# Pooled attention and a gated convolution on one core: the division cut in two, the scale moved into the keys, and a new order for every engine

## The chip, the core and the metric

The kernel runs on one core of a Trainium2 chip. Its engines are TensorE (PE, with its weight loads shown as PEld), VectorE (DVE), ScalarE (ACT), GpSimd (POOL) and SyncE (SP), each with its own program that it works off in order; semaphores join them, and DMA queues are fed from POOL, SP and ACT. The metric is device time in microseconds, the median of several runs. Matmul results land in PSUM, which this kernel uses as eight banks of 128 x 512 fp32.

## What is computed

Eight batches, each with eight heads of 576 rows of 64. Keys and values are averaged over groups of eight rows (72 are left), each query row is scored against the 72 pooled keys of its head, and the softmax of the scores weights the pooled values. The heads side by side are a 576 x 512 activation per batch, which goes through a gated network:

```python
k_p = k.reshape(B, H, Sp, 8, D).mean(axis=3); v_p = v.reshape(B, H, Sp, 8, D).mean(axis=3)
scores = scale * np.matmul(q, k_p.transpose(0, 1, 3, 2))          # scale = 1 / sqrt(64)
attn = np.exp(scores - np.max(scores, axis=-1, keepdims=True))
attn = attn / (np.sum(attn, axis=-1, keepdims=True) + 1e-09)
x = heads_side_by_side(np.matmul(attn, v_p))                      # (8, 576, 512)
h = np.maximum(x @ w_in, 0.0)                                      # (8, 576, 1024)
conv_out = sum(conv_w[k] * shifted(h, k - 1) for k in range(3))    # along the 576 rows
out = (h * sigmoid(conv_out)) @ w_out                              # (8, 576, 512)
```

Inputs and output are fp32 in memory; the kernel computes in bf16 with fp32 sums.

## The kernel before

Batches go in four groups of two (g = 0 to 3). A batch has 576 rows, nine chunks of 64, so a group is cut into nine tiles of 128 query rows (group 0, whose batches are kept apart at the seam, into ten). In the text below b is a batch, t a tile, fb one of eight blocks of 128 of the 1024 hidden columns, f4 a half of these.

*Loads.* POOL issues one casting DMA after another (q in `load_q`, L272; v L305 and L308; keys of a whole group L279; w_in L315, w_out L323). The first batch's keys and part of its queries come raw through SP (L287) and are cast by DVE and ACT (L294). Buffers are few (one for keys, four for q, three for v), so an issue waits until the buffer's former content has been read, and the rest of POOL's queue waits behind it.

*Preparation.* For batches 0 and 1, PE pools the keys with a matrix `pm` of ones (L406, L416). For the others DVE adds the eight rows (`pool_pair`, L439) and PE turns the sums with `pick`, a rearranged identity (L445), or with `ident` itself in the last group (L468). ACT or DVE copies the result out of PSUM into `kT`. PE turns the queries (L516, L520) and ACT or DVE copies them into `qT` (L534); the last group's are turned by DMA. DVE pools the values (L486, L490) into `vm`, beside which a column of eights gives the row sums.

*Attention of one tile.* `att_scores` on PE (L582 in 64 x 64 pieces, L595 in 128 x 128), the row maxima on DVE (`att_max`, L608), the shift by the maximum (`att_shift`, on PE L628 in group 0, on DVE L620 in the others), the exponential on ACT (`att_exp`, L646) with the factor 1/64 as its scale, a turn on PE with a copy (L657, L671) or by DMA (L666), the product with the values on PE (`att_values`, L682). Its result fills two PSUM banks: eight heads of 64 columns and a sum each. `att_divide` on DVE then takes the reciprocals of the eight sums (L695) and multiplies (L697), which frees the two banks. A turn on PE and a copy (L714, L722), or a DMA, puts the tile into `xT`.

*The network of one batch.* PE makes a block of 128 hidden columns (`ffn_in`, L727, eight matmuls of 288 columns into two banks), ACT takes the relu of half of it (L736). The convolution runs along the rows in one of two ways: on PE (`ffn_conv`, L889, pieces of 64 x 64 with diagonal matrices) followed by a tanh on ACT (L914); or, for the pairs (b, f4) in `TAPS`, as three taps: ACT the middle one (L862), DVE the two outer ones (L864), ACT the tanh (L869). With tanh for the sigmoid, DVE adds one and multiplies by `hT`: `ffn_gate` (L925, L927) and `ffn_times` (L935) on the first way, both in `ffn_tap_gate` (L875, L876) on the second. PE multiplies with w_out (`ffn_out`, L943, eight matmuls of 512 columns a tile), ACT or DVE copies (L954), SP or ACT stores (L966).

*What sets the order.* Nothing is ordered by the code's loops. They call `add(...)`, which makes a list of some 900 steps, each with the engines that may do it. Three tables then fix everything: `ORDER` is the sequence of the steps (a step's number doubled, plus one where its second engine does it, so that a copy may be ACT's or DVE's; -1 is a fill, a matmul on a zeroed tile whose result nobody reads, L399), `FORMS` tells whether scores and turns are cut into small pieces, and `PLACES` which buffer or PSUM bank a step gets. `tg`, the accumulator of the taps, has three buffers, `e` six, `x` four.

```python
for n in self.ORDER:
    o = spares.pop(0) if n < 0 else self.ops[n // 2]
    o.engine = list(o.engines)[0 if n < 0 else n % 2]
```

## Time and profile before

| | us |
|---|---|
| median of 3 runs | 217.13 (217.02 to 217.79) |
| span of the profiled execution | 216.5 |
| its time outside the span | not given; the runs' median is 0.63 above the span |
| PE busy (matmuls) | 201.9 |
| DVE busy | 193.2 |
| ACT busy | 162.7 |
| POOL busy | 41.5 |

Durations below are from that one profiled execution; busy time is the union over an engine's instructions. A matmul that waits in PE's queue counts as busy, so 93% of PE is not PE at its peak. Lines of groups read: line, engine, operation, tiles, shapes, count, then busy us, mean ns of one, then idle time of the engine just before them and what ended most of it. In lists of instructions by time the first two numbers are the start and the length in us, and the bracket holds the idle time before and what ended it. In the chain of waits the numbers are start and length.

### The profile page before, as it was taken

To read this page: it belongs to the slowest core of one execution; us is meant where nothing else is said; L and a number is where in the kernel's file an instruction comes from. 1 tells how busy PE (TensorE), PEld (TensorE's weight loads), DVE (VectorE), ACT (ScalarE), POOL (GpSimd) and SP (SyncE) were. 2 spreads that over 40 slices of the span, in tenths; PEclk is the share of its full clock that TensorE was granted. 3 is DMA by queue.
4 is the path that set the end of the run, shared out by engine and by line. 5 is a ranking of instruction groups with operands and counts; after the bars stand their busy time and mean duration, and the time that the engine had idled before them with its cause. 6 is when DMAs were issued, how large, how long until landed. Compare 5 with 4: busy or idle time off the path is not lost.

```text
span 216.5 us, 6617 instructions
## 1 busy us (share of the span) xinstructions
PE 201.9 (93%) x2753; PEld 137.0 (63%) x2753; DVE 193.2 (89%) x334; ACT 162.7 (75%) x278; POOL 41.5 (19%) x78
## 2 busy tenths in 40 slices
PE   7599999969999999999999899989999999999992
PEld 3557778855788776766776675665656666654451
DVE  7598989999999999999999799999899999998621
ACT  2548885896998887787497594878979999997420
POOL 8644330050052101000000030002201210370000
PEclk9799999999999999999999999999999999999999
DMA  6999999999999999969687634576347745602685
GB/s 210 227 207 209 206 207 208 210 205 206 207 205 206 154 153 179 158 164 165 131 111 100 136 74 89 58 156 148 78 104 153 158 100 123 145 0 51 169 242 171
DMA packets 48833, 33.46 MB, mean 155 GB/s; under 512 B 28300, under 2 KB 43812, under 8 KB 48804
## 3 DMA queue, kind: packets, MB, share of 16 engines
q0 software_dynamic: 15216, 15.40, 43.5%
q1 hardware_dynamic: 32512, 16.13, 36.6%
q10 hardware_dynamic: 1076, 1.52, 2.5%
q8 instruction: 21, 0.34, 0.7%
q14 instruction: 8, 0.07, 0.1%
HBM read 32.52 MB, written 9.44 MB: 194 GB/s over the span
## 4 chain that ended last, share of the span: by engine, by line
PE 45%; DVE 34%; issue 6%; ACT 6%; DMA 5%; SPq 2%; DVEq 0%
PE psum L943 20%; PE psum L727 16%; DVE negm L608 7%; DVE x L697 6%; DVE sd L620 4%; DVE gT L935 4%; DMA hT<-in_k_dram 3%; DVE v L486 3%; DVE gT L927 3%; PE psum L889 2%; DMA out_dram<-osb 2%; DVE r L695 2%; PE psum L682 2%; ACT e L646 2%; DVE gT L925 1%
## 5 line engine op out<-in xcount | busy, mean ns | idle before, releaser
L727 PE MATMUL psum<-xT,w_in_sb 128*128 128x288 bf16 x512 | 74.1, 286 | 2.2 <-DMA xT<-x 1.1
L943 PE MATMUL psum<-w_out_sb,gT 128*128 128x512 bf16 (+1 forms) x296 | 69.5, 374 | 0.7 <-DVE gT L935 0.6
L727 PEld LDWEIGHTS <-w_in_sb 128*128 128x128 bf16 x512 | 47.9, 98 | 19.1 <-issue 2.0
L736 ACT ACTIVATE hT<-psum 128x576 bf16<-128x576 f32 x64 | 40.3, 650 | 14.0 <-PE psum L727 13.4
L943 PEld LDWEIGHTS <-gT 128*128 128x128 bf16 x296 | 27.3, 98 | 26.5 <-issue 0.9
L864 DVE SCALAR_TENSOR_TENSOR tg<-hT,convw,tg 128x576 f32<-128x576 bf16 x48 | 37.6, 815 | 0.5
L608 DVE TENSOR_REDUCE negm<-psum 128x8 f32<-128x576 f32 (+2 forms) x37 | 27.5, 752 | 2.3 <-PE psum L582 1.6
L697 DVE TENSOR_TENSOR x<-psum,r 128x512 bf16<-128x512 f32 (+1 forms) x37 | 25.6, 691 | 1.4
L811 POOL COPY hT<-hT 128x126 bf16<-128x126 bf16 x16 | 7.5, 467 | 97.6 <-ACT hT L736 80.1
L620 DVE TENSOR_TENSOR sd<-psum,negm 128x576 f32<-128x576 f32 x27 | 20.2, 753 | 0.5
L682 PE MATMUL psum<-vm,eT 128*128 128x130 bf16 (+5 forms) x240 | 18.9, 222 | 1.1 <-DVE x L697 0.7
L646 ACT ACTIVATE e<-sd 128x576 bf16<-128x576 f32 x27 | 18.2, 685 | 1.3 <-DVE sd L620 1.1
L954 ACT COPY osb<-psum 128x512 f32<-128x512 f32 x27 | 15.7, 585 | 4.4 <-PE psum L943 4.2
L889 PE MATMUL psum<-hT,dw 64*64 64x288 bf16 (+2 forms) x608 | 18.7, 261 | 0.1
L682 PEld LDWEIGHTS <-eT 128*128 128x128 bf16 (+1 forms) x240 | 15.3, 100 | 5.4 <-DMA eT<-e 1.2
L862 ACT ACTIVATE tg<-hT,convw 128x576 f32<-128x576 bf16 x24 | 18.1, 772 | 0.1
L889 PEld LDWEIGHTS <-dw 64*64 64x64 bf16 x608 | 14.8, 107 | 4.6 <-issue 3.7
L869 ACT ACTIVATE gT<-tg 128x576 bf16<-128x576 f32 x24 | 16.3, 683 | 0.7 <-DVE tg L864 0.5
L914 ACT ACTIVATE gT<-psum 128x576 bf16<-128x576 f32 x20 | 12.9, 651 | 3.9 <-PE psum L889 2.7
L914 ACT ACTIVATE tg<-psum 128x576 bf16<-128x576 f32 x20 | 13.0, 652 | 2.6 <-PE psum L889 1.4
L935 DVE TENSOR_TENSOR gT<-gT,hT 128x2304 bf16<-128x2304 bf16 x10 | 13.5, 1352 | 0.1
L486 DVE TENSOR_TENSOR v<-v 128x1280 bf16<-128x1280 bf16 (+2 forms) x24 | 13.0, 540 | 0.2
(84 smaller groups left out, 234.2 us busy)
## 6 DMA issues: line engine op xcount, KB each, us to landing
out_dram<-osb SPq DMA_DIRECT2D x54, 128.0 KB, 2.4
v<-in_v_dram POOLq DMA_DIRECT2D x8, 512.0 KB, 13.1
qp<-in_q_dram POOLq DMA_DIRECT2D x7, 576.0 KB, 14.4
kk<-in_k_dram POOLq DMA_DIRECT2D x3, 1152.0 KB, 14.6
out_dram<-qp ACTq DMA_DIRECT2D x10, 128.0 KB, 2.7
hT<-in_k_dram SPq DMA_DIRECT2D x2, 576.0 KB, 5.0
w_in_sb<-in_moe_w_in_dram POOLq DMA_DIRECT2D x2, 512.0 KB, 14.2
w_out_sb<-in_moe_w_out_dram POOLq DMA_DIRECT2D x1, 1024.0 KB, 24.7
```

What stands on the lines that cost most here:

```text
L608: nc.vector.tensor_reduce(out=a["m"][0:rows], in_=a["s"][0:rows, :, 0:2 * KW].rearrange("p a (h s) -> p a h s", s=Sp), axis=AX.X, op=OP.ma ...
L620: nc.vector.tensor_tensor(out=a["d"][0:rows], in0=a["s"][0:rows, :, 0:2 * KW].rearrange("p a (h s) -> p a h s", s=Sp), in1=a["m"][0:rows]. ...
L646: nc.scalar.activation(out=dst, in_=src, func=ACT.Exp, scale=1.0 / (POOL * 8.0),)
L682: nc.tensor.matmul(out=a["o"][lo:hi, h // 4, (h % 4) * (D + 1):(h % 4 + x1 - x0) * (D + 1)], lhsT=a["eT"][:, j, lo:hi], rhs=buf("vm", b)[: ...
L697: nc.vector.tensor_tensor(out=a["x"][0:rows].rearrange("p (a h d) -> p a h d", a=2, d=D), in0=ov[:, :, :, 0:D], in1=r[0:rows].unsqueeze(3) ...
L727: nc.tensor.matmul(out=banks(ps)[:, j, 0:SC], lhsT=w_in_block(dc, fb), rhs=buf("xT", g)[:, dc, i * S + j * SC:i * S + (j + 1) * SC], start ...
L736: nc.scalar.activation(out=h_of(b)[:, fb].rearrange("p (a s) -> p a s", a=2), in_=banks(ps)[:, :, 0:SC], func=ACT.Relu, scale=0.5,)
L864: nc.vector.scalar_tensor_tensor(out=acc, in0=h, scalar=w, in1=acc, op0=OP.mult, op1=OP.add)
L889: nc.tensor.matmul(out=banks(pss[r ^ c])[c * D:(c + 1) * D, j, lo:hi], lhsT=dw[r * D:(r + 1) * D, tap * n_fb + fb, :], rhs=hT[r * D:(r + 1 ...
L914: nc.scalar.activation(out=t.rearrange("p (a s) -> p a s", a=2), in_=banks(ps)[:, :, 0:SC], func=ACT.Tanh, scale=0.5,)
L935: nc.vector.tensor_tensor(out=gate, in0=gate, in1=h_of(b)[:, four], op=OP.mult)
L943: nc.tensor.matmul(out=bank(ps)[0:rows, columns], lhsT=buf("gT", g)[:, fb, t * P:t * P + rows], rhs=w_out_sb[:, fb, columns], start=(fb == 0),
```

## The change

- `att_divide` becomes two steps. `att_invert` takes the reciprocals on DVE; the multiply is a step of its own, which DVE does as before or ACT does as eight activations of 64 columns, one a head, each with its reciprocal as scale. `ORDER` gives four of the 37 multiplies to ACT.
- `ffn_tap_gate` keeps only the addition of one; the product becomes a step of its own (`ffn_times`).
- The factor 1/64 leaves the exponential. The pooling matrix is filled with it in place of 1.0, and a scaled identity `ident_k` (one more small DVE instruction) is what `pick` is made of and what the last group's keys are turned with.
- `ORDER`, `FORMS` and `PLACES` are new throughout. There are 40 fills for 17, 21 of them ahead of PE's first real matmul (14 before). Of the first batches' turns and scores, other ones are cut small: 252 small query turns for 216, 336 small score pieces for 320. DVE copies two of the large `qT` blocks (five before), ACT eight (five).
- A variant of the exponential, eight activations with the maximum as bias, is added but used nowhere (`EIGHT` is empty).

```diff
@@ class Graph
+    EIGHT = ()
     ORDER = (
-        0, 10, 12, 24, 16, -1, 4, 44, -1, 28, 8, -1, 36, -1, 14, -1, -1, 32, -1, -1,
...
+        0, 10, 24, 16, 4, 44, 28, 8, 36, 12, 14, 32, 46, 3, -1, -1, -1, -1, -1, 48,
...
@@ constants
+    KSCALE = 1.0 / (POOL * 8.0)
+    ident_k = const.tile([P, P], BF16, name="ident_k")
@@ clear_pool_matrix
-        nc.vector.memset(pm[0:TB, :, 0:Sp], 1.0)
+        nc.vector.memset(pm[0:TB, :, 0:Sp], KSCALE)
@@ build_pick
+        nc.vector.tensor_scalar(out=ident_k, in0=ident, scalar1=KSCALE, scalar2=None, op0=OP.mult)
...
-                    in_=ident.rearrange("p (s a hh f e) -> p s a hh f e", s=2, a=2, hh=2, f=2)[:, :, :, hh, f],
+                    in_=ident_k.rearrange("p (s a hh f e) -> p s a hh f e", s=2, a=2, hh=2, f=2)[:, :, :, hh, f],
@@ turn_keys
-                    rhs=ident[:, i * D:(i + 1) * D],
+                    rhs=ident_k[:, i * D:(i + 1) * D],
@@ att_exp
             func=ACT.Exp,
-            scale=1.0 / (POOL * 8.0),
@@ division
+    def att_invert(g, t):
+        nc.vector.reciprocal(out=buf("r", g, t)[0:rows_of(g, t)], in_=att_heads(g, t)[:, :, :, D])
+
+    def att_divide(g, t, engine):
...
+        if engine == "ACT":
+            for n in range(H):
+                nc.scalar.activation(
+                    out=a["x"][0:rows, n * D:(n + 1) * D],
+                    in_=ov[:, n // 4, n % 4, 0:D],
+                    func=ACT.Identity,
+                    scale=r[0:rows, n // 4, n % 4:n % 4 + 1],
+                )
+            return
@@ ffn_tap_gate
         nc.vector.tensor_scalar(out=gate, in0=gate, scalar1=1.0, scalar2=None, op0=OP.add)
-        nc.vector.tensor_tensor(out=gate, in0=gate, in1=h_of(b)[:, four], op=OP.mult)
@@ add_att
-        o = add(dve(0.2, 0.69), key, lambda: att_divide(g, t), after=[o], uses=[x, rr, big])
+        o = add({"DVE": 0.115}, key, lambda: att_invert(g, t), after=[o], uses=[rr, big])
+        o = add({"DVE": 0.61, "ACT": 0.82}, key, None, after=[o], uses=[x, rr, big])
+        o.emit = lambda o=o: att_divide(g, t, o.engine)
@@ add_ffn
-            gated = add(dve(0.78, 1.39), w, lambda f4=f4: ffn_tap_gate(b, f4), after=tanh, uses=[htok[b], gtok[g]])
+            o = add(dve(0.78), w, lambda f4=f4: ffn_tap_gate(b, f4), after=tanh, uses=[gtok[g]])
+            gated = add(dve(1.39), w, lambda f4=f4: ffn_times(b, f4), after=[o], uses=[htok[b], gtok[g]])
```

The lines of the changed kernel are shifted, by 10 to 34; the reciprocal is L716 there, the multiply L731 on DVE and L724 on ACT, the pooling steps L450 and L497, the relu L770. Three places of the order:

DVE in group 1, before: after the first pooling step of the next group's keys (L439 `kk`), two divisions, each reciprocal (into `r`) ahead of its multiply (into `x`), then the maximum of another tile (`negm`) and its shift (`sd`).

```order
L439 TENSOR_TENSOR kk_76<-kk_76 128x9x256
L695 RECIPROCAL r_111<-psum 128x8
L697 TENSOR_TENSOR x_108<-psum,r_111 128x512
L695 RECIPROCAL r_109<-psum 128x8
L697 TENSOR_TENSOR x_105<-psum,r_109 128x512
L608 TENSOR_REDUCE negm_95<-psum 128x8
L620 TENSOR_TENSOR sd_127<-psum,negm_95 128x576
```

The same place now:

```order
L450 TENSOR_TENSOR kk_77<-kk_77 128x9x256
L716 RECIPROCAL r_110<-psum 128x8
L716 RECIPROCAL r_111<-psum 128x8
L731 TENSOR_TENSOR x_106<-psum,r_110 128x512
L692 COPY eT_103<-psum 128x640
...
L619 TENSOR_REDUCE negm_96<-psum 128x8
L631 TENSOR_TENSOR sd_128<-psum,negm_96 128x576
```

The two reciprocals stand ahead of the first multiply, and the second multiply (of `r_111`) is no longer on DVE. It is on ACT, while batch 1's relus (into `hT`) and the last tanh results of batch 0 (into `gT`, `tg`) run; before, ACT had at that place

```order
L914 ACTIVATE tg_118<-psum 128x576
L914 ACTIVATE gT_119<-psum 128x576
L722 COPY xT_113<-psum 128x4x128
L736 ACTIVATE hT_115<-psum 128x576
L671 COPY eT_104<-psum 128x640
```

and now

```order
L946 ACTIVATE gT_120<-psum 128x576
L946 ACTIVATE tg_119<-psum 128x576
L770 ACTIVATE hT_116<-psum 128x576
L756 COPY xT_114<-psum 128x4x128
L724 ACTIVATE x_108<-psum,r_111 128x64 x8
L770 ACTIVATE hT_116<-psum 128x576
L668 ACTIVATE e_99<-sd_127 128x576
```

The eight activations of one division stand between two relus, whose PSUM banks PE waits for.

POOL's queue at the start, before: keys and q of batch 1, four clears of the ends of `hT`, w_in's first half, q of batch 2, w_in's second half, v of batch 1.

```order
L272 DMA qp_72<-in_q_dram 128x4x320
L305 DMA v_85<-in_v_dram 128x4x512
...
L272 DMA kk_76<-in_k_dram 128x4x576
L272 DMA qp_73<-in_q_dram 128x4x576
L806 MEMSET hT_114 128x8
...
L315 DMA w_in_sb_66<-in_moe_w_in_dram 128x4x512
L272 DMA qp_74<-in_q_dram 128x4x576
L315 DMA w_in_sb_67<-in_moe_w_in_dram 128x4x512
```

Now:

```order
L282 DMA qp_74<-in_q_dram 128x4x320
L315 DMA v_87<-in_v_dram 128x4x512
...
L282 DMA kk_77<-in_k_dram 128x4x576
L282 DMA qp_74<-in_q_dram 128x4x576
L282 DMA qp_73<-in_q_dram 128x4x576
L325 DMA w_in_sb_67<-in_moe_w_in_dram 128x4x512
L325 DMA w_in_sb_68<-in_moe_w_in_dram 128x4x512
```

The clears have gone far back, q of batch 2 stands ahead of both halves of w_in, and q of batch 1 goes into the buffer that q of batch 0 has (`qp_74`; two buffers before), so its issue, with all behind it, waits until PE has turned batch 0's queries.

More of the change, by code (lines that the diff above doesn't have):

```diff
@@ L1113, in add_pair @@
             t = token("ps", n=2)
-            o = add({"PE": 0.26}, key, lambda b=b, t=t: turn_keys(b, t), after=[prev, c0], uses=[t, kk[g]], mode=HALF, count=36)
+            o = add({"PE": 0.26}, key, lambda b=b, t=t: turn_keys(b, t), after=[prev, picked], uses=[t, kk[g]], mode=HALF, count=36)
             c = add(either(0.76, 0.71), key, None, after=[o], uses=[t, ktok[b]])
@@ L1209, in add_att @@
         o = add(dve(0.75), key, lambda: att_max(g, t), after=[o], uses=[ng, s])
-        if shift_by_dve(g, t):
+        if by_head(g, t):
+            o = add({"ACT": 0.9}, key, lambda: att_exp(g, t), after=[o], uses=[e, s, ng, lim])
+        elif shift_by_dve(g, t):
             sd = token("sd", g, t)
@@ L1340, in add_out @@
             key += nudge("ot", 9 * g + t)
-            osb, free = (token("late", g, t), qdone[7, 0]) if g == 3 else (token("osb", g, t), [])
+            osb, free = (token("late", g, t), [x for n in range(4, B) for x in qdone[n, 0]]) if g == 3 else (token("osb", g, t), [])
             need = [a for x in groups[g][0:i + 1] for a in gdone[x]]
```

28 lines of the change are left out of this document (20 added, 8 removed), and 140 rows, old and new, of tables (ORDER, PLACES).

## The prediction

> **What bounds the kernel now.** I read the page first, then the chain of waits, then busy time by stage, and cut the stages where the chain changes engine: first real matmul (7.83 us), first row maximum (12.35), first block of the input product (27.5), first block of the output product (48.9), the place where the chain stays on PE (144.7), the last run of output matmuls (199.1).
>
> ```profile
> span 216.5 us, 6617 instructions
> ...
> PE 201.9 (93%) x2753; PEld 137.0 (63%) x2753; DVE 193.2 (89%) x334; ACT 162.7 (75%) x278; POOL 41.5 (19%) x78
> ...
> PE 45%; DVE 34%; issue 6%; ACT 6%; DMA 5%; SPq 2%; DVEq 0%
> ```
>
> ```profile
> 7.83:12.35 4.52, 4.38 (x89) 3.98 (x89) 1.72 (x11) 2.42 (x5) 2.98 (x8) 0.62 1.21 179
> 12.35:27.50 15.15, 13.72 (x293) 9.89 (x293) 14.01 (x28) 11.28 (x20) 4.92 (x8) 1.00 1.23 207
> 27.50:48.90 21.40, 19.35 (x391) 15.89 (x390) 19.75 (x36) 17.47 (x32) 4.93 (x7) 1.00 1.24 208
> 48.90:144.70 95.80, 92.36 (x1465) 65.91 (x1465) 92.50 (x161) 75.19 (x130) 10.07 (x19) 1.00 0.90 147
> 144.70:199.10 54.40, 54.39 (x437) 33.00 (x438) 51.97 (x73) 48.70 (x83) 11.87 (x23) 1.00 0.49 109
> 199.10:216.50 17.40, 13.15 (x68) 6.47 (x68) 6.83 (x10) 4.89 (x9) 0.00 (x0) 1.00 0.64 181
> ```
>
> Columns: stretch, length, busy time of PE, PEld, DVE, ACT and POOL, then granted clock, DMA share, GB/s. DVE works 92.50 of 95.80 us in the long middle stage; with the clipped gaps between its instructions it is saturated, and the chain there runs mostly over it. From 144.7 us PE is busy 54.39 of 54.40 and the chain no longer leaves it:
>
> ```profile
> 145.24 0.98 PE psum L727 x8
> 146.22 0.86 PE psum L943 x4
> ...
> 199.10 13.16 PE psum L943 x68
> ```
>
> So four input matmuls cost 0.49 us and four output matmuls 0.86 when nothing stops them. How much PE loses in the middle stage shows in the same two lines there:
>
> ```profile
> 48.90:144.70 95.80, 41.39 (x284) 26.19 (x284) 1.00 0.90 147
> 48.90:144.70 95.80, 24.07 (x96) 8.39 (x96) 1.00 0.90 147
> ```
>
> L727's 284 matmuls would take 34.8 us at 0.49 a four and spend 41.39; L943's 96 would take 20.6 and spend 24.07. With the 3.44 us in which PE is plainly idle (95.80 less 92.36), PE could finish this stage at least 3.4 and at most 13.5 us sooner, if DVE delivered. That is what a relief of DVE can buy; behind 144.7 us it buys nothing by itself.
>
> **What the change takes from DVE.** Today each division is a reciprocal (L695) and a multiply (L697) that waits for it:
>
> ```profile
> 96.67 0.76 DVE L620 TENSOR_TENSOR sd<-psum,negm 128x576 f32<-128x576 f32 x1
> 97.34 0.20 DVE L695 RECIPROCAL r<-psum 128x8 f32<-128x8 f32 x1
> 97.57 0.69 DVE L697 TENSOR_TENSOR x<-psum,r 128x512 bf16<-128x512 f32 x1
> 98.18 0.20 DVE L695 RECIPROCAL r<-psum 128x8 f32<-128x8 f32 x1
> 98.41 0.69 DVE L697 TENSOR_TENSOR x<-psum,r 128x512 bf16<-128x512 f32 x1
> ```
>
> Starts are what count: after L620 (0.76 long) the next starts 0.67 later, after L697 0.61 later, so independent neighbours overlap by 0.08 to 0.09 us; the multiply, which needs the reciprocal, starts 0.23 after it. A reciprocal with something else behind it should cost 0.20 - 0.09 = 0.11, so 0.12 less (estimate; bounds 0 and 0.23).
>
> In the new order 23 of the 37 reciprocals still stand directly ahead of their own multiply: nothing gained. 14 stand apart: 14 x 0.12 = 1.7 us. Four of these have their multiply on ACT: 4 x 0.61 = 2.4. The gate's add and product (L875, L876) pay the same toll,
>
> ```profile
> 198.30 0.76 DVE L875 TENSOR_SCALAR gT<-gT 128x2304 bf16<-128x2304 bf16 x1 [0.89 <-ACT gT L869]
> 199.10 1.36 DVE L876 TENSOR_TENSOR gT<-gT,hT 128x2304 bf16<-128x2304 bf16 x1
> 201.80 1.36 DVE L935 TENSOR_TENSOR gT<-gT,hT 128x2304 bf16<-128x2304 bf16 x1
> ```
>
> 0.80 from start to start where 0.67 would do; four of six come apart: 0.5. The other copies change engines in the new order; I counted forms in both orders and price DVE's at the mean less 0.09:
>
> ```profile
> L534 DVE COPY qT<-psum 128x1152 bf16<-128x1152 bf16 x5 | 3.8, 758 | 1.3 <-PE psum L520 1.3
> L431 DVE CAST kT<-psum 64x144 bf16<-64x144 f32 x2 | 0.6, 312 | 2.6 <-PE psum L406 2.6
> L671 DVE COPY eT<-psum 128x640 bf16<-128x640 bf16 x3 | 1.5, 484 | 0.4 <-ACT kT L431 0.4
> L954 DVE COPY qp<-psum 128x512 f32<-128x512 f32 x3 | 2.1, 689 | 6.0 <-PE psum L943 6.0
> L954 DVE COPY qp<-psum 128x256 f32<-128x256 f32 x2 | 0.8, 424 | 0.7 <-PE psum L943 0.7
> L534 ACT COPY qT<-psum 128x1152 bf16<-128x1152 bf16 x5 | 5.5, 1124 | 1.7 <-PE psum L520 1.7
> L431 ACT CAST kT<-psum 64x144 bf16<-64x144 f32 x2 | 0.5, 270 | 1.1 <-DVE kT L431 1.1
> L722 ACT COPY xT<-psum 128x256 bf16<-128x256 bf16 x2 | 0.7, 371 | 0.0
> ```
>
> Three qT copies leave (-2.0), two kT casts leave (-0.4), one osb copy comes (+0.6, as L954's 512), a half block leaves (-0.3), one eT copy of 640 and one of half that come (+0.6), and the small rest (an xT copy half the size, a cast of q, the scaled identity) is about +0.3, my estimate. Sum: -1.7 - 2.4 - 0.5 - 2.0 - 0.4 + 0.6 - 0.3 + 0.6 + 0.3 = **-5.8 us of DVE**. Some 0.8 of it (two qT copies and the kT casts against the newcomers) lies before 48.9 us, some 4.2 in the middle stage, 0.8 behind. Of the 4.2 I let four fifths reach the end, -3.4: it is the plain idle time of PE, which is the lower of the two bounds above; ends 0 and -4.2. The 0.8 before 48.9 I count at -0.3, since loads pace that stage (below).
>
> **What ACT gets.** Three qT copies (+3.0), 32 new activations of 64 columns. No row has that size; the two small ones differ by 0.9 ns a column (371 less 270 over 112), so one takes about 0.20 us, 0.11 if it overlaps its neighbour as on DVE: 0.9 us a division; without overlap 1.6, at the 270 ns of the nearest row 2.2. ACT idles 20 us in the middle stage, which hides its share there, but only 5.70 behind 144.7, where two of the four divisions come: +0.5 for relus and tanhs that come late to PE or to the last gate, between 0 and +2.5 (the ACT rival below).
>
> By the Trainium skill, "ScalarE: Activation LUTs", Rules for kernel authors, a multiply belongs on VectorE, and an ACTIVATE is to be budgeted at about 0.3 us plus 0.83 ns an element, which makes a division 2.8 us (estimate from that page); the 270 ns row is already below its fixed part, so here the trace decides. By the page the two late divisions would put 5.6 us on ACT, 55.3 in all for the stage, which at 95% of the time is 3.8 us more than it has, and the sum would end at 216.7.
>
> **The start.** 21 fill matmuls (L399) now precede the first real one, against 14, and the first real one is a turn of q, not the pooling of k.
>
> ```profile
> 1.23 4.57 PE L399 MATMUL psum<-gT 128*128 128x448 bf16 x14 [1.23 <-DVE gT L1052]
> 7.83 0.97 PE L406 MATMUL psum<-gT,kk 128*64 128x144 bf16 x18 [2.03 <-DVE gT L347]
> 10.45 1.52 PE L516 MATMUL psum<-ident,qp 128*64 128x128 bf16 x28
> ...
> 8.00:9.00 1.00, 1.00 (x26) 0.99 (x22) 0.16 (x1) 0.84 (x1) 0.00 (x0) 0.61 1.26 163
> 9.00:10.00 1.00, 0.87 (x17) 0.64 (x14) 0.15 (x1) 0.96 (x3) 0.63 (x5) 0.50 1.06 138
> ```
>
> After a pause of 2.03 us the clock fell to half, and the stretch 7.83 to 12.35 ran at 0.62: it lost 4.52 x 0.38 = 1.7 us. Seven more fills at 0.33 (4.57 over 14) end near 8.1 and close the pause. Against that, the pool matrix is built after the four clears of kT (1.2 us later) and a real matmul may stand behind fills. I take -0.5 between -1.7 and +1.
>
> By the Trainium skill, "TensorE: Matmul & The Clock Gate", What's actually happening, the clock drops after an idle window of about 3.4 us; here 2.03 us sufficed. By its rule, work behind sustained activity runs at full rate, the start would give the whole -1.7, and the sum would be 1.2 us lower.
>
> Why not more: loads arrive just in time.
>
> ```profile
> w_out_sb<-in_moe_w_out_dram POOLq DMA_DIRECT2D x1, 1024.0 KB, 24.7
> ...
> 22.06 0.89 POOL L323 DMA_DIRECT2D w_out_sb<-in_moe_w_out_dram  x1 [1.16 <-DMA w_in_sb<-in_moe_w_in_dram]
> ...
> 48.92 1.04 PE L943 MATMUL psum<-w_out_sb,gT 128*128 128x512 bf16 x4 [0.61 <-DVE gT L935]
> ```
>
> w_out lands at 22.06 + 24.7 = 46.8, 2.1 us ahead of its first use, and the DMA share stays at 1.2 until then. On POOL's queue q of batch 1 now takes the buffer of q of batch 0, so it waits for PE, with q of batch 2 and both halves of w_in behind it; the queue's own backlog covers that unless PE's first turns end later than today's 11.97 (10.45 + 1.52). The pooling scale moves into the matrix and the picking identity: the same instructions with another constant, one small one more, hidden at the start. Exp without a factor: nothing.
>
> **Sum.** -3.4 - 0.3 + 0.5 - 0.5 = -3.7 on a span of 216.5: 212.8. No row tells this execution's time outside the span; the runs' median is 217.13, 0.63 above it, which I add: **213.4 us**.
>
> **Rivals.**
>
> More (210): the start gives its 1.7 and the middle stage the whole 4.2, ACT costs nothing: 217.13 - 4.2 - 0.8 - 1.7 = 210.4. For it: PE's 13.5 us upper bound. Against: PE must then lose almost nothing to latency.
>
> Hidden (216.6): PE's lost time in the middle stage is latency of the steps, not lack of DVE; the relief becomes idle DVE time and only the start's -0.5 remains. For it: issue has 6% of the chain. Against: DVE's 92.50 of 95.80.
>
> Banks (219.0, slower): a division holds two of the eight PSUM banks until its multiply is done. Set apart, it holds them one more DVE instruction, about 0.75 us; on ACT about 0.95 (0.9 and a relu of 0.65 ahead, less 0.61). The list of waits (total, times, longest) shows PE waiting for just this:
>
> ```profile
> PE psum L595 <- DVE x L697: 0.9, 1, 0.9
> ...
> PE psum L682 <- DVE x L697: 0.7, 1, 0.7
> ```
>
> 10 x 0.75 + 4 x 0.95 = 11.3 us if every hold stopped PE; half makes 5.6, so 219.0. It decides from two fifths on (4.8 of 11.3 carry 213.4 over 218.2). Against: PE has other work queued between, and only two such waits show.
>
> ACT (215.4): at 2.2 us a division ACT needs 48.70 + 4.4 + 1 (one more copy, two more store issues, estimated) = 54.1 of the stage's 54.40. It holds 90% there today; at 95% the stage takes 56.9, which puts +2.5 in the place of my +0.5. It decides from about 1 us a division on. For it: 270 ns for a 64x144 cast. Against: ACT idles 5.70 us there.
>
> **Numbers.** Likeliest 0.47 (its own range 211 to 216), more 0.13, hidden 0.15, banks 0.20, ACT 0.05. About 0.5%, or 1.1 us, is what a measurement of this kernel can tell from no change: 216.0 to 218.2. Faster: 0.47 + 0.13 + 0.02 of hidden + 0.02 of ACT = 0.64. Same: 0.10 of hidden + 0.03 of ACT = 0.13. Slower: 0.20 + 0.03 of hidden = 0.23. The range runs from 208.5, below which little of "more" lies, to 219.0, the middle of "banks": some 0.12 is outside.
>
> **What the new profile would show.** DVE's busy time near 187.5; L534 twice on DVE; reciprocals with a foreign neighbour 0.11 to 0.12 apart from it; the 32 activations at about 0.2 us; a granted clock near 1.00 from 8 to 12 us; PE's last run of output matmuls starting near 195. I am wrong if the clock falls again and the first row maximum comes after 12.35, if PE's waits on the division's buffer grow beyond 4 us, or if DVE is relieved and merely idles.

## The result and the profile after

The changed kernel takes 216.59 us (median of 20 runs, 215.10 to 217.61) where the kernel before, measured with it, takes 217.37 (20 runs, 216.87 to 219.27): a ratio of 0.9952, 95% interval 0.9935 to 0.9969, so 0.8 us faster. The forecast was 3.7 us faster. The sign was right, the size was not.

From the page of the profiled execution: the span, busy time, the granted clock in 40 slices, and the chain by engine.

```profile
span 215.9 us, 6780 instructions
...
PE 203.4 (94%) x2810; PEld 139.0 (64%) x2810; DVE 188.9 (87%) x329; ACT 171.2 (79%) x312; POOL 43.8 (20%) x78
...
PEclk9999999999999999999999999999999999999996
...
PE 34%; DVE 22%; ACT 21%; issue 8%; DMA 6%; ACTq 4%; POOL 2%; SPq 0%; DVEq 0%
```

DVE has 4.3 us less to do, ACT 8.5 more. The chain has left PE and DVE for ACT (21% for 6) and DMA, and ACT's queue of DMA issues (ACTq) is new in it. The clock no longer falls at the start.

All executions of the changed kernel last about 1.7 us longer than their span; the profiled one, 217.61 with a span of 215.9, is the slowest of its 20. If the kernel before has the same 1.7 outside its span, its profile is of an execution of about 218.2, slow for its kind too. Profile against profile the change gains 0.6 us, median against median 0.8.

Busy time by stage, cut at the same places as before (first row maximum, first input block, first output block, 145, last run of output matmuls); columns as in the prediction:

```profile
0.00:13.03 13.03, 9.27 (x112) 5.02 (x112) 8.53 (x34) 5.72 (x10) 5.95 (x15) 1.00 0.90 199
13.03:29.25 16.22, 15.25 (x343) 11.74 (x343) 14.35 (x30) 11.40 (x20) 8.82 (x12) 1.00 1.22 204
29.25:49.95 20.70, 19.84 (x412) 15.60 (x403) 17.90 (x29) 18.19 (x32) 4.89 (x11) 1.00 1.23 207
49.95:145.00 95.05, 93.95 (x1492) 68.74 (x1488) 91.73 (x162) 81.14 (x150) 11.25 (x21) 1.00 0.91 151
145.00:197.27 52.27, 51.93 (x411) 31.33 (x404) 49.65 (x68) 50.53 (x97) 12.85 (x20) 1.00 0.57 120
197.27:215.90 18.63, 13.13 (x68) 6.56 (x67) 6.70 (x10) 4.17 (x8) 0.00 (x0) 0.91 0.54 142
```

The first output block starts at 49.95, where it started at 48.92. Three numbers tell the whole story, and all runs below are measured by them: the start of the first output block, the stretch from there to the end of PE's last matmul, and the rest of the span.

| | first output block | stretch to PE's end | PE's end to the end |
|---|---|---|---|
| before | 48.92 | 163.33 | 4.27 |
| after | 49.95 | 160.45 | 5.51 |
| difference | +1.03 | -2.88 | +1.24 |
| forecast | -0.8 | -2.9 | 0 |

In these two profiles the middle did what was forecast, and the gain was given back at the two ends, 1.0 and 1.2 us. Each column is read from one execution a kernel, and the ends scatter: the four kernels with the same start (this one, e4, e5 and e6 below) put the first output block at 48.88 to 50.45, and the ten with this tail (this one, e1 to e3, e5 to e8, e11 and e15) leave 4.81 to 6.00 us behind PE's end, where three in the old order besides the kernel before (e9, e10 and e14) leave 4.32 to 4.41. So the tail's direction is sure, the start's rests on e1 below, and both sizes are rough: the medians, 0.8 us apart, fit a loss at the start of about 0.8 when the middle and the end are taken as in the table.

The start, from POOL's timeline (start, length, instruction, idle time before and what ended it) and the list of waits:

```profile
3.15 1.64 POOL L341 TENSOR_SCALAR_AFFINE_SELECT gT<-gT 64x648 bf16<-64x648 bf16 x2 [1.09 <-DVE gT L352]
4.74 0.96 POOL L282 DMA_DIRECT2D qp<-in_q_dram  x1
...
13.12 1.48 POOL L282 DMA_DIRECT2D qp<-in_q_dram  x2 [5.20 <-DVE qT L545]
```

```profile
PE psum L527 <- DMA qp<-in_q_dram: 1.8, 1, 1.8
```

POOL waits 1.09 us for DVE to clear the pool matrix. Every load on POOL's queue stands behind that, the first, the second part of batch 0's q, is issued at 4.74 (3.59 before), and PE, at full clock, waits 1.8 us for it. It lands at 11.79 and the first row maximum starts at 13.03. In all eleven executions with these 21 fills (this one, e1 to e8, e12 and e13) the first row maximum starts 1.24 to 1.25 us after that landing, which comes between 9.94 and 12.59 us. So the landing of that load sets the start, and not PE's clock, as long as that is up.

The end, from the timeline:

```profile
197.27 13.13 PE L975 MATMUL psum<-w_out_sb,gT 128*128 128x512 bf16 x68 [0.19 <-ACT tg L946]
...
209.07 0.59 ACT L986 COPY qp<-psum 128x512 f32<-128x512 f32 x1 [2.60 <-DMA out_dram<-qp]
...
210.98 0.37 ACT L986 COPY qp<-psum 128x256 f32<-128x256 f32 x1 [1.32 <-PE psum L975]
211.38 1.77 ACTq L998 DMA_DIRECT2D out_dram<-qp  x3
```

PE's last run takes 13.13 us as before (13.16), but three stores follow one another on ACT until 213.15, 2.75 us after PE's end; in the kernel before the last store was issued 1.37 us after it.

The new instructions, by form:

```profile
L724 ACT ACTIVATE x<-psum,r 128x64 bf16<-128x64 f32 x32 | 7.0, 327 | 0.6 <-DVE r L716 0.6
L545 DVE COPY qT<-psum 128x1152 bf16<-128x1152 bf16 x2 | 1.5, 758 | 0.2 <-PE psum L531 0.2
```

A small activation lasts 327 ns, and the starts of neighbours lie 0.20 us apart, so a division occupies ACT for 1.6 us (1.75 until its last result), not the 0.9 of the forecast.

### The profile page after: what moved, and what is told of

Read it like the earlier page. It is cut to its first block, busy times and chain, and to the rows that moved or that the text cites. A ratio compares the mean times of both kernels' runs of the same rounds, so it can differ in the third digit from the quotient of the medians.

```text
span 215.9 us, 6780 instructions
## 1 busy us (share of the span) xinstructions
PE 203.4 (94%) x2810; PEld 139.0 (64%) x2810; DVE 188.9 (87%) x329; ACT 171.2 (79%) x312; POOL 43.8 (20%) x78
## 3 DMA queue, kind: packets, MB, share of 16 engines
q10 hardware_dynamic: 1236, 1.78, 3.2%
## 4 chain that ended last, share of the span: by engine, by line
PE 34%; DVE 22%; ACT 21%; issue 8%; DMA 6%; ACTq 4%; POOL 2%; SPq 0%; DVEq 0%
PE psum L761 13%; PE psum L975 6%; DVE tg L898 6%; PE psum L921 4%; ACT hT L770 4%; PE psum L703 4%; ACT tg L896 4%; ACTq L998 4%; DMA qp<-in_q_dram 3%; DVE x L731 3%; DVE negm L619 3%; ACT gT L903 3%; DVE gT L967 2%; ACT e L668 2%; ACT osb L986 2%
## 5 line engine op out<-in xcount | busy, mean ns | idle before, releaser
L761 PE MATMUL psum<-xT,w_in_sb 128*128 128x288 bf16 x512 | 71.7, 286 | 0.6
L975 PE MATMUL psum<-w_out_sb,gT 128*128 128x512 bf16 (+1 forms) x296 | 68.5, 373 | 0.2 <-ACT tg L946 0.2
L770 ACT ACTIVATE hT<-psum 128x576 bf16<-128x576 f32 x64 | 40.9, 659 | 9.3 <-PE psum L761 9.0
L845 POOL COPY hT<-hT 128x126 bf16<-128x126 bf16 x16 | 9.5, 591 | 99.2 <-ACT hT L770 90.8
L731 DVE TENSOR_TENSOR x<-psum,r 128x512 bf16<-128x512 f32 (+1 forms) x33 | 22.6, 687 | 0.8
L967 DVE TENSOR_TENSOR gT<-gT,hT 128x2304 bf16<-128x2304 bf16 x16 | 21.8, 1360 | 0.3
L896 ACT ACTIVATE tg<-hT,convw 128x576 f32<-128x576 bf16 x24 | 18.8, 791 | 0.3
L921 PEld LDWEIGHTS <-dw 64*64 64x64 bf16 x608 | 15.3, 107 | 4.4 <-issue 3.3
L545 ACT COPY qT<-psum 128x1152 bf16<-128x1152 bf16 (+2 forms) x10 | 10.3, 1030 | 4.3 <-PE psum L527 4.3
```

What stands on the lines that cost most here:

```text
L731: nc.vector.tensor_tensor(out=a["x"][0:rows].rearrange("p (a h d) -> p a h d", a=2, d=D), in0=ov[:, :, :, 0:D], in1=r[0:rows].unsqueeze(3) ...
L761: nc.tensor.matmul(out=banks(ps)[:, j, 0:SC], lhsT=w_in_block(dc, fb), rhs=buf("xT", g)[:, dc, i * S + j * SC:i * S + (j + 1) * SC], start ...
L770: nc.scalar.activation(out=h_of(b)[:, fb].rearrange("p (a s) -> p a s", a=2), in_=banks(ps)[:, :, 0:SC], func=ACT.Relu, scale=0.5,)
L896: nc.scalar.activation(out=acc, in_=h, func=ACT.Identity, scale=w)
L921: nc.tensor.matmul(out=banks(pss[r ^ c])[c * D:(c + 1) * D, j, lo:hi], lhsT=dw[r * D:(r + 1) * D, tap * n_fb + fb, :], rhs=hT[r * D:(r + 1 ...
L967: nc.vector.tensor_tensor(out=gate, in0=gate, in1=h_of(b)[:, four], op=OP.mult)
```

## The experiments

ORDER holds a step's number doubled, plus one for its second engine; PLACES the buffers. Most edits are a few numbers in these tables; the diffs show the numbers that change with a few neighbours, and a row can be cut short. "Stretch" is the second column above. The columns of time within the span come from one profiled execution a kernel. Ratios are to the kernel before on the same chip; e5 to e8 ran on a chip on which the changed kernel was not run, so their distance from it goes over the kernel before.

| run | median us | ratio to before (95%) | first output block | stretch | PE's end to end |
|---|---|---|---|---|---|
| e1_pm_first | 215.59 | 0.9900 (0.9880-0.9919) | 47.85 | 160.27 | 5.47 |
| e2_q1_own_buffer | 216.68 | 0.9966 (0.9942-0.9991) | 48.65 | 160.38 | 5.73 |
| e3_start | 215.25 | 0.9885 (0.9865-0.9906) | 47.85 | 160.42 | 5.04 |
| e4_tail | 216.72 | 0.9959 (0.9934-0.9984) | 48.88 | 160.41 | 5.17 |
| e5_div_on_dve | 218.78 | 1.0062 (1.0033-1.0092) | 50.45 | 163.12 | 4.81 |
| e6_late_div_on_dve | 217.82 | 0.9993 (0.9960-1.0026) | 49.48 | 161.35 | 5.36 |
| e7_adjacent | 217.92 | 1.0006 (0.9975-1.0038) | 51.23 | 161.35 | 5.87 |
| e8_unrelieved | 220.69 | 1.0153 (1.0108-1.0197) | 50.64 | 163.86 | 6.00 |
| e9_old_order_new_code | 217.46 | 1.0011 (0.9983-1.0038) | 48.95 | 163.54 | 4.34 |
| e10_old_order_act_division | 220.53 | 1.0159 (1.0115-1.0203) | 49.06 | 165.12 | 4.41 |
| e11_pm_first_14_fills | 216.07 | 0.9938 (0.9906-0.9970) | 47.93 | 161.35 | 5.51 |
| e12_start_and_tail | 215.22 | 0.9903 (0.9876-0.9931) | 48.38 | 160.08 | 5.11 |
| e13_tail_balanced | 214.49 | 0.9874 (0.9849-0.9900) | 47.84 | 160.51 | 4.44 |
| e14_old_order_act_later | 220.97 | 1.0177 (1.0145-1.0209) | 49.03 | 166.49 | 4.32 |
| e15_pm_first_9_fills | 219.34 | 1.0094 (1.0057-1.0131) | 49.81 | 162.26 | 5.06 |

### The start: e1, e2, e3

e1, the clear of the pool matrix ahead of the clears of kT:

```diff
-        0, 10, 24, 16, 4, 44, 28, 8, 36, 12, 14, 32, 46, 3,
+        0, 10, 24, 16, 4, 44, 28, 8, 12, 36, 14, 32, 46, 3,
```

> The pool matrix is cleared ahead of the four clears of kT, as before the change; nothing else differs from the changed kernel. Late-start theory: the second part of q of batch 0 is issued near 3.6 us in place of 4.74 and lands near 10.5 in place of 11.79, so PE's wait for it (1.8 us) shrinks, but q of batch 1 still waits for PE's turns, some 1.2 us earlier than now: all loads move 1.0 to 1.3 us ahead, DVE's idle time ahead of the first block of the output product falls by about 1 us, and the time by 0.5 to 1.0 us against the changed kernel (ratio to the kernel before 0.991 to 0.993). Rival, that the loads have slack there: within 0.3 us of the changed kernel (0.9952).

e2, another buffer for q of batch 1:

```diff
-        1, 3, 1, 3, 6, 2, 7, 2, 3, 0, 5, 2,
+        1, 3, 2, 3, 6, 2, 7, 2, 3, 0, 5, 2,
```

> q of batch 1 gets a buffer of its own (the one that lies idle until the last group), so its issue no longer waits for PE's turns of batch 0; the pool matrix stays late. Late-start theory: POOL issues it near 7.7 us in place of 13.1, w_in and w_out land 1 to 2 us sooner, DVE's idle time ahead of 50 us falls by about 1 us, time 0.5 to 1.0 us below the changed kernel (ratio 0.991 to 0.993). Rival, that the queue's backlog covers the wait, as the prediction had it: loads land within 0.3 us of where they do, and the time is that of the changed kernel (0.9952).

e3 makes both edits:

```diff
-        0, 10, 24, 16, 4, 44, 28, 8, 36, 12, 14, 32, 46, 3,
+        0, 10, 24, 16, 4, 44, 28, 8, 12, 36, 14, 32, 46, 3,
...
-        1, 3, 1, 3, 6, 2, 7, 2, 3, 0, 5, 2,
+        1, 3, 2, 3, 6, 2, 7, 2, 3, 0, 5, 2,
```

> Both of the first two edits. Late-start theory: first row maximum near 11.8, first block of the output product near 48.5 in place of 50.0, time 1.3 to 2.0 us below the changed kernel (ratio 0.986 to 0.989). Rival: nothing beyond 0.3 us; then the two lost microseconds of DVE ahead of 50 us come from the order of the work itself and not from loads.

Two swapped numbers are worth 1.1 us (0.9900 against 0.9952; 2.1 us between the two profiles at the first output block). POOL's and PE's timeline of e1:

```profile
3.59 0.89 POOL L282 DMA_DIRECT2D qp<-in_q_dram  x1
```

```profile
47.85 1.47 PE L975 MATMUL psum<-w_out_sb,gT 128*128 128x512 bf16 x6
```

The first load leaves at 3.59 again and the first output block comes 1.07 us ahead of the kernel before. In the four executions with the matrix first and 21 fills (e1, e3, e12, e13) the load lands at 9.94 to 10.17 and PE waits for it 0.23 us at most; in the four kernels with the changed start it lands at 10.55 to 12.59 and PE waits 0.4 to 2.6. That settles the start: the pool matrix, ahead of the load that PE waits for. The second edit does nothing that can be measured, alone (0.9966 with an interval that holds 0.9952) or on top of e1 (47.85 both times). In e2 POOL issues q of batch 1 at 7.92 in place of 13.12, and it lands at 20.35 in place of 20.59: the queue's backlog covers the wait, as the prediction had it. Of e2's two theories the rival holds.

### What the fills are worth: e11, e15

Both are e1 with fills taken out ahead of the first real matmul, 7 and 12 of 21:

```diff
-        -1, -1, -1, -1, -1, 42, -1, -1, -1, -1, -1, -1, 34, -1, -1, 38, -1, -1, 20, 62,
+        -1, -1, -1, -1, -1, 42, -1, -1, -1, -1, 34, 38, 20, 62,
```

> e1 without the last 7 of its 21 fills ahead of the first real matmul. Clock theory: the fills end near 5.8 us, PE then idles some 1.8 us, the granted clock falls to half for 2 to 3 us as in the kernel before, the first row maximum comes near 12.2 in place of 11.2, and the time is 0.8 to 1.7 us above e1 (ratio 0.994 to 0.998). Rival, that loads set the start whatever the clock: the clock falls, but the first row maximum moves by under 0.4 and the time by under 0.4 (ratio 0.989 to 0.992).

```diff
-        -1, -1, -1, -1, -1, 42, -1, -1, -1, -1, -1, -1, 34, -1, -1, 38, -1, -1, 20, 62,
+        -1, -1, -1, -1, 42, 34, 38, 20, 62,
```

> e1 with 9 of the 21 fills ahead of the first real matmul: fills end near 4.3 us, PE pauses some 3.2 us. Clock theory: the granted clock falls to half from 8 to about 11 us, the first row maximum comes at 12.0 to 12.6 in place of 11.2, the first output block at 48.6 or later in place of 47.85, the time 0.6 us or more above e1 (ratio 0.993 or more). Rival, that loads set the pace there at either clock: the first output block within 0.3 us of 47.85, the ratio 0.989 to 0.992.

The turns of q at the start (PE's groups by form from 6 to 13 us), in e11 and then in e15:

```profile
L527 PE MATMUL psum<-ident,qp 128*64 128x128 bf16 x36 | 1.4, 220 | 1.6 <-DVE qp L304 1.6
```

```profile
L527 PE MATMUL psum<-ident,qp 128*64 128x128 bf16 x36 | 2.3, 313 | 2.8 <-DVE qp L304 2.8
```

In e11, after a pause of 1.6 us, a turn takes 220 ns, as in e1; in e15 it takes 313. So e11 could not tell the two theories apart (its clock stayed up, which I had not expected), and e15 could: the slow clock costs 1.96 us at the first output block (49.81 for 47.85). It does so not through PE's turns alone: q of batch 1, which shares a buffer with batch 0's, is issued at 13.38 in place of 11.27.

That the turns are slow is sure; that the pause of 2.8 us slowed them is not. The fills themselves are slow at first and fast later. Those of the changed kernel from 1.7 to 3.9 us, those from 4.9 to 6.9, then all nine of e15 ahead of its pause:

```profile
L410 PE MATMUL psum<-gT 128*128 128x448 bf16 x8 | 3.2, 577 | 1.2 <-DVE gT L1084 1.2
```

```profile
L410 PE MATMUL psum<-gT 128*128 128x448 bf16 x11 | 2.2, 353 | 0.0
```

```profile
L410 PE MATMUL psum<-gT 128*128 128x448 bf16 x9 | 3.5, 578 | 1.2 <-DVE gT L1084 1.2
```

e15 has only fills of the slow kind, so its clock had most likely not come up yet when the pause began. The clock theory holds in this order, with the loads in time: a clock that is down at the first real matmuls costs about 2 us, near the prediction's 1.7. It need not be so elsewhere: in the old order e14, below, has the clock up (turns of 219 ns) and its first output block at 49.03 all the same, where the kernel before, with the clock down, has 48.92. e11 and e15 lose a further 1.0 and 1.9 us near 90 us, in the same place, where PE stands ahead of a turn (L531) for nothing that the profile shows; that part is not explained.

### The relief of DVE: e5, e6, e7, e8

e5 gives the four multiplies back to DVE, e6 only the two of group 3:

```diff
-        1015, 1201, 1635, 1875
+        1014, 1200, 1634, 1874
```

> All four multiplies that the change gave to ACT are back on DVE, at the same places; nothing else. The measure is the time from the first block of the output product to PE's last matmul, 163.3 us in the kernel before and 160.3 to 160.5 in the changed kernel and the four runs that only altered its ends. Relief theory (DVE's time is what bounds the middle): DVE gets 4 x 0.61 = 2.4 us back, the stretch grows by 1.5 to 2.4, to 162 to 163. ACT theory (from 158 us the chain runs over ACT, which the divisions of 1.56 us each overload): the two early ones cost as in the relief theory, the two late ones gain about as much, and the stretch stays within 0.5 of 160.4.

```diff
-        1635, 1875
+        1634, 1874
```

> Only the two late multiplies (group 3, tiles 1 and 5) go back to DVE. ACT theory: ACT gets 2 x 1.56 = 3.1 us back where the chain runs over it, the last run of output matmuls starts 0.5 to 1.3 us sooner, the stretch from the first output block to PE's end is 159.1 to 159.9, and the time falls by as much. Relief theory: DVE is at 95% there too, the stretch grows by 0.6 to 1.2, to 161.0 to 161.6.

e7 puts the reciprocals that stand apart back ahead of their multiplies; one of ten places on DVE:

```diff
-L716 RECIPROCAL r_110<-psum 128x8
 L631 TENSOR_TENSOR sd_129<-psum,negm_96 128x576
+L716 RECIPROCAL r_110<-psum 128x8
 L731 TENSOR_TENSOR x_106<-psum,r_110 128x512
```

> The ten reciprocals that stand apart from a multiply on DVE go back directly ahead of it. By the prediction's price DVE gets 10 x 0.12 = 1.2 us more to do. Relief theory: DVE's busy time or its short waits grow by 1.2, the stretch from the first output block to PE's end by 0.6 to 1.2, to 161.0 to 161.6. Rival, that placing them apart is worth nothing (a reciprocal with a foreign neighbour takes as long from start to start): within 0.2 us of 160.4.

e8 does e5 and e7 and takes three qT copies back from ACT:

```diff
-        227, 239, 267
+        226, 238, 266
```

> The new order without its relief of DVE: the four multiplies back on DVE, the ten reciprocals back ahead of their multiplies, and three large qT copies (one each of batches 2, 3 and 5) back from ACT to DVE. DVE gets 2.4 + 1.2 + 2.0 = 5.6 us back. Relief theory: the stretch from the first output block to PE's end grows by 3 to 5 us, to 163.5 to 165.5, at or above the kernel before, and the time to 219 or more (ratio 1.005 to 1.02). Rival, that the new order of PE is what gained, not the relief: within 1.5 us of 160.4 (ratio below 1.00).

The relief theory holds throughout. The stretch grows by 2.67 us in e5 (2.4 of DVE), by 0.90 in e6 (1.2 of DVE) and by 3.4 in e8. e8 as a whole is slower than the kernel before, but by its two ends: its stretch, 163.86, is about the old order's 163.33. In the profile of e7 the clock fell at 13 us, which no other execution with 21 fills shows, so I go by its ratio: 0.54% over the changed kernel, 1.2 us for ten reciprocals, DVE's busy time 0.8 up; its stretch grows by 0.90. The stretch is 161.35 in e6, e7 and, without any edit to the divisions, in e11. That is chance in e11, whose loss is the one step near 90 us; set against the changed kernel from the first output block on, e6 is within 0.3 us of it until the first of its two divisions (150.3 us), 0.6 behind at the next input block (158.6) and 0.7 to 0.9 behind after the second (169.4). e5 falls back in the same way behind each of its four divisions (66.2, 106.6, 150.3 and 169.4 us), to 0.4, 1.5, 2.4 and 2.7 us. The ACT theory falls with e6: from 158 us on the chain of the changed kernel runs mostly over ACT, and yet the time grows when ACT gets 3.0 us back (168.2 busy for 171.2).

### Order and relief apart: e9, e10, e14

e9 is the changed code with the sequence, engines, buffers and banks of the kernel before:

```diff
-        0, 10, 24, 16, 4, 44, 28, 8, 36, 12, 14, 32, 46, 3, -1, -1, -1, -1, -1, 48,
+        0, 10, 12, 24, 16, -1, 4, 44, -1, 28, 8, -1, 36, -1, 14, -1, -1, 32, -1, -1,
...
```

> The changed code in the old order: division in two steps that stand one behind the other, all multiplies on DVE, gate in two steps likewise, the scale in the keys; the sequence, engines, buffers and banks of the kernel before. If the order is all that counts: DVE's busy time 193.0 to 193.6, the stretch from the first output block to PE's last matmul 163.1 to 163.5, ratio 0.998 to 1.002. If the code itself does something (the scale in the keys, the missing factor in the exponential): outside of that. Its profile is also a second sight of where the old order stands at the first output block (48.92 in the profile before).

e10 gives ACT the same four multiplies in that order:

```diff
-        1014, 1200, 1634, 1874
+        1015, 1201, 1635, 1875
```

> As e9, and the multiplies of the same four tiles as in the changed kernel (group 1 tile 8, group 2 tile 3, group 3 tiles 1 and 5) on ACT; nothing else of the new order. Relief theory: DVE has 2.4 us less to do, the stretch from the first output block to PE's end falls from 163.3 by 1.0 to 2.4, to 161 to 162.3, ratio 0.989 to 0.996. Rival, that only an order made for it lets PE use the relief: within 0.5 of 163.3, ratio 0.998 to 1.002; or, if ACT's 1.56 us a division holds up relus PE waits for, above 163.8.

e14 puts each of them one instruction later on ACT; the first of the four places:

```diff
+L690 COPY eT_103<-psum 128x640
 L722 ACTIVATE x_106<-psum,r_110 128x64 x8
-L690 COPY eT_103<-psum 128x640
 L754 COPY xT_114<-psum 128x4x128
```

> e10, with each of the four divisions one instruction later on ACT: behind the eT copy (group 1 tile 8), a relu (group 2 tile 3), a tanh and a middle tap (group 3). Place theory: in e10 the first division held up an eT copy, PE's product with the values came late, and DVE's next reciprocals idled 0.30 + 0.74 us for it; with the copy ahead that goes, the step of 1.2 us at 66 to 74 us falls below 0.4, DVE's waits for L701 fall from 3.6 to under 2 us, and the stretch from the first output block to PE's end is 164.0 or less (165.1 in e10, 163.5 in e9), ratio 1.000 to 1.010. Load theory: ACT's 1.6 us a division hold up something else just as much, the stretch stays at 164.8 or more, ratio 1.012 or more.

The code alone, the scale in the keys with it, changes nothing (1.0011). The four multiplies on ACT, without the new order, are a loss of 3.1 us: they make the kernel slower by 1.6% (medians of four runs; the stretch grows by 1.58 over e9's). The rest of the relief, the reciprocals set apart and the copies moved to ACT, was not tried in the old order. DVE's timeline of e10 at the first division:

```profile
66.69 0.76 DVE L617 TENSOR_REDUCE negm<-psum 128x8 f32<-128x576 f32 x1 [0.47 <-PE psum L591]
67.48 0.76 DVE L629 TENSOR_TENSOR sd<-psum,negm 128x576 f32<-128x576 f32 x1
68.54 0.21 DVE L714 RECIPROCAL r<-psum 128x8 f32<-128x8 f32 x1 [0.30 <-PE psum L701]
68.78 0.69 DVE L729 TENSOR_TENSOR x<-psum,r 128x512 bf16<-128x512 f32 x1
70.21 0.21 DVE L714 RECIPROCAL r<-psum 128x8 f32<-128x8 f32 x1 [0.74 <-PE psum L701]
```

DVE is relieved of 0.61 us and idles 1.5 (0.47, 0.30 and 0.74, the first ahead of the place). I took the eT copy behind the division for the cause; e14 moves it ahead and the loss stays (step of 1.2 us as before, stretch 166.49). The place theory falls for the two places tried, and the load theory stands. In e14 PE waits 2.8 us in all for banks that the division on ACT holds, about the size of its 2.95 us over e9's stretch; in e10 these waits are 0.8 us, half its loss, and in the changed kernel there are none.

```profile
PE psum L919 <- ACT x L722: 1.0, 2, 0.5
PE psum L973 <- ACT x L722: 0.9, 1, 0.9
PE psum L701 <- ACT x L722: 0.9, 2, 0.5
```

Which neighbours make a division on ACT harmless was not tried one by one, and why e10 loses is open; what is shown is that the same four gain 2.7 us of the stretch in one order and lose 1.6 of it in the other.

### The tail: e4, e12, e13

e4 moves a copy to DVE and a store to SP:

```diff
-        2104, 2112, 2107, 2111, 2109, 2114, 2116, 2119,
+        2104, 2112, 2106, 2110, 2109, 2114, 2116, 2119,
```

> In the last 3 us one copy of half a tile goes from ACT to DVE and one half-tile store from ACT to SP; nothing else. Tail theory: after PE's last matmul ACT's queue is busy issuing stores and holds the last but one copy, so the last store leaves 2.7 us after PE's end where 1.4 would do; with the edit it leaves 1.0 to 1.3 us sooner, and the time falls by as much (ratio 0.990 to 0.991). Rival, that the end is set by the landing of stores issued earlier, since the DMA queues are full there: within 0.3 us.

e12 is e3 and e4 with two other buffers:

```diff
-        6, 2, 4, 1, 6, 7, 5, 5, 3, 2, 2, 0, 4, 4,
+        6, 2, 4, 1, 6, 7, 5, 5, 3, 2, 0, 0, 4, 1,
```

> e3 with e4's edit at the end, and with the two last output tiles in buffers that nobody has used (0 and 1 of the eight late ones, which the new order leaves empty while it uses 2 and 4 twice). In e4 the first of the last two copies still waited for the store of its buffer's former content to land (209.25) and began at 209.44, the same as without. Buffer theory: without that wait it begins about 0.8 us sooner, from PE's last matmul to the end 4.2 to 4.5 us in place of 5.0 to 5.5, and the time is 0.6 to 1.0 us below e3 (ratio 0.984 to 0.986). Rival, that the landing of the stores already under way sets the end: 5.0 or more, ratio as e3 (0.9885).

e13 gives three tiles' stores to SP, two of them behind SP's older ones:

```diff
-        1942, 1937, 1945, 1947, 1953, 1956, 1958, 1955, 1706, 1472, 1456, 1939, 1961, 1448, 1698, 1963, 2096,
-        2080, 2082, 2074, 2084, 2103,
+        1942, 1937, 1945, 1947, 1953, 1956, 1958, 1706, 1472, 1456, 1961, 1448, 1698, 1938, 1954, 1963, 2096,
+        2080, 2082, 2074, 2084, 2102,
```

> e12, and the stores of three whole tiles (batch 6 tiles 0 and 2, batch 7 tile 7) move from ACT's queue to SP's, which is idle for 6 us there; SP's older stores stay ahead of them. ACT-queue theory: the copies on ACT no longer wait behind stores of 0.6 us each, the last store leaves 1.0 to 1.4 us after PE's last matmul in place of 1.95, PE's end to the end of the span is 4.1 to 4.5 us in place of 5.1, time 0.6 to 1.0 us below e12 and e3 (ratio about 0.985). Rival, landing: the last store leaves sooner, but the span ends 4.9 to 5.2 us after PE all the same. (Of e12's two buffers, number 1 had indeed been free; number 0 had been used once, early.)

e4's copy moved to DVE and began no sooner. DVE's timelines of e4, e12 and e13:

```profile
209.44 0.82 DVE L986 COPY qp<-psum 128x256 f32<-128x256 f32 x2 [1.12 <-PE psum L975]
```

```profile
207.69 0.42 DVE L986 COPY qp<-psum 128x256 f32<-128x256 f32 x1 [0.20 <-PE psum L975]
```

```profile
207.59 0.42 DVE L986 COPY qp<-psum 128x256 f32<-128x256 f32 x1 [0.19 <-PE psum L975]
```

In e4 both halves are copied at 209.44, behind PE's end at 209.29; the idle time is put down to PE, but in the chain of waits the landing of an earlier store, whose buffer the new order uses again, ends at 209.25. With another buffer (e12) the first half goes 0.77 us ahead of PE's end (208.46). That alone moved nothing: ACT's queue was still busy and the last store left 1.95 us after PE's end. With the stores shared (e13) 4.44 us remain behind PE, within 0.2 of the old order, and the time falls to 214.49, ratio 0.9874. The intervals of e12 and e13 overlap, and those of e3 and e13 as well, so for the last step the 0.67 us in the profile is the better evidence; e13's 4.44 lies below all ten executions with the unchanged tail, e4's 5.17 and e12's 5.11 do not. That two causes hid each other, a buffer used twice and too many stores on one queue, is an inference: sharing the stores without the other buffers was not tried.

e13 has the lowest ratio: 2.7 us below the kernel before, with its start mended, its tail mended, and the middle as the change made it.

## Why the prediction was right and wrong

- **The middle: right, by offsetting errors.** -3.4 and +0.5 were forecast, -2.88 came. The relief was smaller than summed (DVE's busy time fell by 4.3, not 5.8; some 0.6 of that are gaps between instructions, which the sum counted and busy time does not), and a division costs ACT 1.6 us, not 0.9. That is the bound without overlap that I named and did not take, but by another road: an activation lasts 327 ns, not 200, and overlaps its neighbour by 0.13. I had scaled by columns from two copies where most of the length is fixed (a relu of 576 columns lasts 659 ns, these of 64 columns 327). On the other side the relief reached the end almost whole (e5: 2.67 us for 2.4 of DVE), not at four fifths, and it also paid behind 144.7 us, where I had said that it buys nothing by itself: e6 charges 0.90 for two late multiplies.
- **The reciprocal's price: right.** With another instruction behind it the next starts 0.114 to 0.125 us later in ten places of the changed kernel, for the 0.11 of the estimate (ahead of a gate it took 0.145 once, ahead of a reciprocal that was not ready 0.31). Ten of them were worth about 1.2 us (e7).
- **The start: the step that failed.** It set "the pool matrix is built after the four clears of kT (1.2 us later)" against PE's regained clock and took -0.5, with -0.3 for relief. The clock did stay up, but the start was not PE's: the matrix stands on POOL ahead of every load, the first of them slipped by 1.15 us, and PE waited for q, whose landing sets the first row maximum. Measured: +1.03 in the profile, the upper bound I had given, and about +0.8 by the medians; -1.07 against the kernel before with the matrix in its old place (e1). I had seen that loads arrive just in time, and did not carry the delay through the queue that issues them. The seven more fills did not end near 8.1 either but at 6.93, since later fills follow one another faster (0.19 us apart) than the mean of 0.33 that I took.
- **q of batch 1 behind PE's turns: right.** The backlog covers it (e2).
- **The tail: the second step that failed, a term put at nothing.** The prediction followed the work up to PE's last run and took what is behind it as unchanged, without a reason. The order of stores there was new as well; it cost 1.24 us in the profile (0.5 to 1.7 over the ten executions with that tail), and e13 ends 1.07 us nearer to PE's end. Start and tail together, about +2 where -0.8 and nothing were put, are what the forecast of -3.7 missed. The 0.63 us outside the span, 1.7 for the changed kernel, shifted the forecast time but not the gain.
- **The rivals.** Banks: not in the new order, where PE's longest wait on a multiply is 0.3 us; in the old order it is what e14 shows for divisions on ACT. ACT: its share of the chain went from 6% to 21%, but e6 shows that DVE still bounds there. Hidden: no, the middle gained; that its 216.6 is the measured time is luck. In the old order the four multiplies were not even hidden, they cost (e10).
- **What the profile was to show.** Two large qT copies on DVE, the clock at 1.00 and the reciprocals came true; the 32 activations start 0.20 us apart but last 0.33; DVE's busy time was 188.9 for 187.5; the last run began at 197.27 for 195; the first row maximum came late (13.03), though not for the clock that I had named as the reason.

## What to carry to other kernels

Follow a moved step through every queue that it stands ahead of: four clears on DVE, 1.22 us together, delayed POOL's first load by 1.15 us and with it everything up to the last store. Relief of the busiest engine and the order are one change: the same four multiplies on ACT gained 2.7 us of the stretch in the order made for them and lost 1.6 in the old one, and without the relief the new order's stretch is no shorter than the old one's (e8). And check what happens behind the last matmul: which queue issues the last stores, and whether a buffer there is used twice.

## What the hardware showed unexpectedly

- **The clock can be down without its record.** In e15 the windows from 8 to 12 us show a granted clock of 1.00, yet a turn takes 313 ns for 220, about what it took in the kernel before (296 on average there, at a recorded 0.50 to 0.61). The first fills of the changed kernel, 577 ns at a recorded 1.00 where later ones take 353, look the same. Durations tell the clock more surely than its record.

```profile
10.00:11.00 1.00, 1.00 (x12) 0.52 (x12) 0.00 (x0) 0.28 (x2) 0.00 (x0) 1.00 1.21 193
```

- **The length of a pause alone does not tell whether the clock falls.** It stayed up behind pauses of 1.55 us (e11), 1.61 (e6), 1.78 (the changed kernel) and 2.60 (e5, whose turns behind it take 221 ns); it fell, by its record, behind 1.95 (e7), 2.00 (e10), 2.03 (before) and 2.35 (e9). The Trainium skill, "TensorE: Matmul & The Clock Gate", What's actually happening, gives a window of about 3.4 us; these pauses are shorter than it and four of them sufficed.

```profile
12.64 0.75 PE L527 MATMUL psum<-ident,qp 128*64 128x128 bf16 x20 [2.60 <-DMA qp<-in_q_dram]
```

- **Small activations overlap more than DVE's instructions.** 327 ns long, they start 0.20 us apart, so 0.13 overlaps, against 0.08 to 0.09 on DVE. The Trainium skill, "ScalarE: Activation LUTs", What ACT_TABLE_LOAD costs, puts an activation with a scale per partition at about 280 ns plus 0.833 ns an element, which makes about 333 ns for 64 (estimate from that page): the trace agrees. Its overlap of about 93 ns is less than the trace's 130.
- **The order runs in lockstep.** The changed kernel and e1 to e4 took 160.27 to 160.45 us for the stretch (e12 and e13 160.08 and 160.51), while their first output blocks lie 2.1 us apart (47.85 to 49.95): what the start loses is carried unchanged to the end. Two executions, in e11 and e15, got out of step once, by 1.0 and 1.9 us, and in the same place; why is open.
